# Small normalisation operations on GpSimd, W1's first pieces split by halves, the first x tile in two halves

## The chip, the cores and the metric

The kernel runs on one core of one Trainium2 chip. The metric is device microseconds of one execution. Before the change the median of three runs is 3407.81 us (3403.24 to 3411.15).

The engines are named as in the profile: PE is TensorE (PEld its weight loads), DVE is VectorE, ACT is ScalarE, POOL is GpSimd, and SP issues the transfers (SPq is its queue). Each engine executes its own instructions in the order in which the program lists them, and waits for other engines and for transfers through semaphores.

## The reference

`x` is 2048 x 1024 in float32. The kernel computes

```python
xn = layernorm(x)                        # over the last axis, eps 1e-5, no gain or bias
q, k, v = split(xn @ wqkv)               # 32 heads of 32
s = softmax(q @ k.T / sqrt(32)) @ v @ wo
h = xn @ w1 + b1                         # 1024 -> 3584
g = silu(mish(h) @ w2)                   # mish(h) = h * tanh(softplus(h))
out = x + s * g
```

Only the beginning matters here: the normalisation of `x`, the first part of `V = xn @ wv`, and the preparation of the first pieces of `w1`.

## The kernel before, in words

Every float32 matrix product is made of three products in a faster format: each operand is split into a high part (a rounded copy) and a low part (what is left), and high x high, high x low and low x high are summed. So each tile that goes into TensorE needs a copy on one engine and a subtraction (`low`) on another.

The tokens are handled in 16 tiles of 128 rows (`NT` = 16). The loop `for t in range(2, NT + 2)` is the first V pass, and a "round" below is one pass of this loop. It runs as a pipeline over tiles:

- `x_load(t)` fetches a 512 KB tile of x into one of five buffers that it shares with the raw tiles of wv. SP issues it, and waits there until the earlier user of that buffer is done.
- `ln_a(t)` on VectorE: two `bn_stats` over 512 columns each, `bn_aggr` to mean and variance, and the variance plus eps.
- `ln_r(t)` on ScalarE: the inverse square root as Ln and then Exp with scale -0.5.
- `ln_b(t)` on VectorE: four operations on 128x1 tiles that refine that root by a step of Newton's and make the bias, -mean x root.
- `ln_x(t)` on ScalarE: one 128x1024 activation that applies scale and bias.
- `ln_t(t)` on TensorE: eight 128x128 transposes into two PSUM tiles `pt`.
- `ln_c(t)`: for each half, ScalarE copies the high part from `pt` into `xc`, and VectorE subtracts the low part into it.
- `v_group(0, t)` on TensorE: 24 matmuls of 256 columns; the transposes of the next tile are placed between the eighth and the ninth (between the twelfth and the thirteenth in the first round).
- `evac()`: ScalarE copies the V tile out of PSUM, and SP issues its store.

In round t the program lists `ln_b(t)`, the matmuls of tile t-2 with the transposes of tile t-1, `ln_c(t-1)`, `ln_x(t)`, the load of tile t+4, `ln_a(t+2)`, `ln_r(t+1)`, `evac` of tile t-2, and then the preparation of w1. That order is the order on each engine's queue.

The preparation of w1 uses idle time and idle space. `w1_first(n, step)` handles the first four pieces of w1 (`W1_0` = 4), each 512 KB raw and 1 MB split. Step 0 is the load into a buffer of its own (SP); then GpSimd makes the high and the low part, four instructions over two halves of the piece; then SP moves the result to DRAM. The split piece is written into a place that isn't needed yet: the low parts of `xc[2]` and `xc[3]`, which hold tiles 8 to 11 and 12 to 15. Pieces 0 and 2 take the part that the first half of `ln_c` writes, pieces 1 and 3 the part that the second half writes, so each move must have read its place before `ln_c(8)` or `ln_c(12)` writes there. Before the change piece n is loaded in round n+2, split in round n+3 and moved in round n+5.

In rounds 9, 11, 13 and 15 SP also issues 1 MB moves of finished parts of `xc` to DRAM (`move_x`), and in rounds 13 to 15 the loads of the raw wv of the second V pass; GpSimd splits these at the end of the loop. The second V pass (512 columns, `vww`, `vwz`, `vwb`) begins after them. Behind it come the third V pass, Q and K with the preparation of w1 and w2, and then attention and the MLP, whose instructions a planner puts in order when the program is built; none of that is touched.

Of the kernel before, what the change touches and what calls it, by code (L numbers as in the profile page):

```python
# [11 lines left out]
AF = mybir.ActivationFunctionType  # L12
ALU = mybir.AluOpType
# [4 lines left out]
S, D, H, DH, F = 2048, 1024, 32, 32, 3584  # L18
P = 128
# [7 lines left out]
W1_0, W1_V = 4, 21  # L27
# [196 lines left out]
def body(ctx: ExitStack, tc: tile.TileContext, x, wqk, wv, wo, w1, b1, w2, out):  # L224
    nc = tc.nc
    x, out = x[0], out[0]
# [45 lines left out]
    def act(out_, in_, fn, bias=None, scale=1.0):  # L272
        nc.scalar.activation(out_, in_, fn, bias=zero if bias is None else bias, scale=scale)  # L273
# [4 lines left out]
    def move(out_, in_, eng=None):  # L278

        (eng or nc.sync).dma_start(out_.bitcast(F32), in_.bitcast(F32))  # L280

    def low(eng, out_, in_, high):

        eng.tensor_tensor(out_, in_, high.bitcast(F32), ALU.subtract)  # L284
# [22 lines left out]
    def v_load(i, half):  # L307
        raw = vp.tile([P, 4, 256], F32, tag="x", name=f"vraw{i}_{half}", bufs=5)
        nc.sync.dma_start(raw, wv[i][:, half * 4:half * 4 + 4])
        return raw  # L310
# [6 lines left out]
    def v_group(p, t, cut=0, between=None):  # L317
        w, first, cols = v_pass[p]
        ps = ps1.tile([P, 512], F32, tag="ps", name=f"v{first}_{t}")
        n = 0  # L320
        for k in range(KT):
            for a, b in THREE:
                if n == cut and between:
                    between()
                nc.tensor.matmul(ps[:, :cols], xc[t // 4][:, a, k, (t % 4) * P:(t % 4 + 1) * P],  # L325
                                 w(b, k), start=n == 0, stop=n == 3 * KT - 1)
                n += 1

        def evac():
            for i in range(cols // 256):  # L330
                st = vp.tile([P, 8, DH], F32, tag="vst", name=f"vst{first + i}_{t}", bufs=6)
                copy(st, ps[:, i * 256:(i + 1) * 256].rearrange("p (h d) -> p h d", d=DH))
                nc.sync.dma_start(vs[first + i][:, t], st)

        return evac
# [5 lines left out]
    def v_wide():  # L341
        tiles = [vp.tile([P, 2, 4, 512], F32R, tag="w", name="vww"),
                 w1p.tile([P, 2, 2, 512], F32R, tag="z0", name="vwz"), big.tile([P, 2, 2, 512], F32R, tag="w", name="vwb")]

        def at(b, k):
            return tiles[0][:, b, k] if k < 4 else tiles[1 + k // 2 - 2][:, b, k % 2]

        def split(i, half, raw):
            r = slice(i * 256, i * 256 + 256)
            if half == 0:  # L350
                v_split([tiles[0][:, a, :, r] for a in range(2)], raw, nc.gpsimd)
            else:
                for n in range(2):
                    v_split([tiles[1 + n][:, a, :, r] for a in range(2)], raw[:, 2 * n:2 * n + 2], nc.gpsimd)

        return at, split
# [2 lines left out]

    def x_load(t):  # L360
        xt = vp.tile([P, D], F32, tag="x", name=f"x{t}", bufs=5)
        nc.sync.dma_start(xt, x[t * P:(t + 1) * P, :])
        return xt

    first_w1 = [p.tile([P, 2, KT, P], F32, tag=tag, name=f"w1f{tag}") for p, tag in ((w1p, "z0"), (big, "w"))]

    def split_w(w, raw, job=False):
        for half in range(2):
            r = slice(half * 4, half * 4 + 4)
            p = w[half] if isinstance(w, list) else w[:, half]  # L370
            (nc.gpsimd if job else nc.vector).tensor_copy(p[:, 0], raw[:, r])
            low(nc.gpsimd if job else nc.vector, p[:, 1], raw[:, r], p[:, 0])

    def w1_first(n, step):
        t, g = xc[2 + n // 2], n % 2
        raw = first_w1[n // 2][:, g]
        w = t[:, 1, 4 * g:4 * g + 4].rearrange("p k n -> p (k n)") \
            .rearrange("p (h a k f) -> p h a k f", h=2, a=2, f=P)
        if step == 0:
            nc.sync.dma_start(raw, w1[n])  # L380
        elif step == 1:
            split_w(w, raw, True)
        else:
            move(w1s[n], w)

    xts = {t: x_load(t) for t in range(2)}
    vraw = [v_load(0, half) for half in range(2)]
    xts[2] = x_load(2)
    stat, tmps = {}, {}

    def ln_a(t):
        xt = xts[t]
        st = vp.tile([P, 2, 6], F32, tag="st", name=f"st{t}", bufs=4)
        mv = vp.tile([P, 2], F32, tag="mv", name=f"mv{t}", bufs=5)
        var = vp.tile([P, 1], F32, tag="var", name=f"var{t}", bufs=5)
        rs = vp.tile([P, 1], F32, tag="rs", name=f"rs{t}", bufs=5)
        for g in range(2):
            nc.vector.bn_stats(st[:, g], xt[:, g * 512:(g + 1) * 512])
        nc.vector.bn_aggr(mv, st)
        nc.vector.tensor_scalar(var, mv[:, 1:2], EPS, None, op0=ALU.add)  # L400
        stat[t] = mv, var, rs

    def ln_r(t):
        mv, var, rs = stat[t]
        act(rs, var, AF.Ln)
        act(rs, rs, AF.Exp, scale=-0.5)

    def ln_b(t):
        mv, var, rs = stat.pop(t)
        tmps[t] = tmp = vp.tile([P, 1], F32, tag="tmp", name=f"tmp{t}", bufs=3)  # L410
        nc.vector.scalar_tensor_tensor(tmp, rs, var, rs, op0=ALU.mult, op1=ALU.mult)
        nc.vector.tensor_scalar(tmp, tmp, -0.5, 1.5, op0=ALU.mult, op1=ALU.add)
        nc.vector.tensor_tensor(rs, rs, tmp, ALU.mult)
        nc.vector.scalar_tensor_tensor(tmp, mv[:, 0:1], -1.0, rs, op0=ALU.mult, op1=ALU.mult)
        tmps[t] = tmp, rs

    def ln_x(t):
        tmp, rs = tmps.pop(t)
        act(xts[t], xts[t], AF.Identity, bias=tmp, scale=rs)

    def ln_t(t):
        xt = xts.pop(t)
        for g in range(2):
            pts_[t, g] = pt = ps1.tile([P, 512], F32, tag="ps", name=f"pt{t}_{g}")
            for k in range(4):
                nc.tensor.transpose(pt[:, k * P:(k + 1) * P], xt[:, (4 * g + k) * P:(4 * g + k + 1) * P], ident)

    def ln_c(t):
        c, r = t // 4, slice(t % 4 * P, t % 4 * P + P)
        for g in range(2):  # L430
            k = slice(4 * g, 4 * g + 4)
            p4 = pts_.pop((t, g)).rearrange("p (k n) -> p k n", k=4)
            copy(xc[c][:, 0, k, r], p4)
            low(nc.vector, xc[c][:, 1, k, r], p4, xc[c][:, 0, k, r])

    pts_ = {}
    ln_a(0)
    ln_r(0)
    ln_b(0)
    ln_x(0)  # L440
    ln_a(1)
    ln_t(0)
    ln_r(1)
    ln_b(1)
    vw, parts_ = v_narrow(0)
    v_pass[0] = vw, 0, 256
    v_split(parts_(0), vraw[0], nc.vector)
    ln_c(0)
    v_split(parts_(1), vraw[1], nc.gpsimd)
    ln_x(1)  # L450
    ln_a(2)
    ln_r(2)
    xts[3] = x_load(3)
    x_parts = iter([(c, k) for c in range(1, NC) for k in range(0, KT, 2)])

    def move_x():
        c, k = next(x_parts)
        move(xs[c][:, :, k:k + 2], xc[c][:, :, k:k + 2])

    for t in range(2, NT + 2):  # L460
        if t < NT:
            ln_b(t)
        evac = v_group(0, t - 2, 12 if t == 2 else 8, (lambda: ln_t(t - 1)) if t <= NT else None)
        if t <= NT:
            ln_c(t - 1)
        if t < NT:
            ln_x(t)
        for m in (4, 5, 6) if t == 2 else (t + 4,):
            if m < NT:
                xts[m] = x_load(m)  # L470
        if t == 2:
            ln_a(3)
        if t + 2 < NT:
            ln_a(t + 2)
        if t + 1 < NT:
            ln_r(t + 1)
        evac()
        for step, n in enumerate((t - 2, t - 3, t - 5)):
            if 0 <= n < W1_0:
                w1_first(n, step)  # L480
        if t == NT - 3:
            vraw = {(i, 0): v_load(1 + i, 0) for i in range(2)}
        elif t in (NT - 2, NT - 1):
            i = t - NT + 2
            vraw[i, 1] = v_load(1 + i, 1)
        if 8 < t < NT and t % 2:
            move_x()
        if t == NT - 1:
            vw, split_wide = v_wide()
            v_pass[1] = vw, 1, 512  # L490
        if t >= NT - 1:
            for i, half in (((0, 0), (1, 0)), ((0, 1),), ((1, 1),))[t - NT + 1]:
                split_wide(i, half, vraw[i, half])
# [9 lines left out]
    def qk_split(f):  # L503
        qkw[f] = w_tile(f"qkw{f}")
        split_w(qkw[f], raws.pop(f))
# [904 lines left out]
    xt, yt = {}, {}  # L1410
# [23 lines left out]
    for c in range(NC):  # L1434
        for s in range(4):
            t = 4 * c + s
            if t + 4 < NT:
                start(t + 4)
            for dh in range(2):
# [5 lines left out]
                if c:  # L1445
                    n = 2 * s + dh
# [53 lines left out]
```

## Time and profile before

| | before |
|---|---|
| median of three runs | 3407.81 us |
| the profiled execution | 3404.78 us, span 3403.0 us |
| PE busy | 3350.0 us (98%) |
| DVE, ACT, POOL busy | 2683.6, 2039.2, 2727.3 us |
| mean granted TensorE clock | 0.998 |
| start of the second V pass's matmuls on `vwz` | 83.15 us |

A row of the timeline gives the start, the duration, the engine, the source line, the operation, the tile written and the tiles read, their shapes, how many instructions are merged in the row, and in brackets how long the engine was idle before it and what ended that wait. A row of the stages gives the stretch, its length, the busy time and number of instructions of PE, PEld, DVE, ACT and POOL, the granted clock, the share of the DMA engines' time and GB/s. A row of groups gives line, engine, operation, tiles, shapes and count, then busy time and mean nanoseconds of one, then the idle time before them. A row of the waits gives who waited for whom: total, times, longest.

### The profile page before, as it was taken

To read this page: it belongs to the slowest core of one execution; us is meant where nothing else is said; L and a number is where in the kernel's file an instruction comes from. 1 tells how busy PE (TensorE), PEld (TensorE's weight loads), DVE (VectorE), ACT (ScalarE), POOL (GpSimd) and SP (SyncE) were. 2 spreads that over 40 slices of the span, in tenths; PEclk is the share of its full clock that TensorE was granted. 3 is DMA by queue.
4 is the path that set the end of the run, shared out by engine and by line. 5 is a ranking of instruction groups with operands and counts; after the bars stand their busy time and mean duration, and the time that the engine had idled before them with its cause. 6 is when DMAs were issued, how large, how long until landed. Compare 5 with 4: busy or idle time off the path is not lost.

```text
span 3403.0 us, 48050 instructions
## 1 busy us (share of the span) xinstructions
PE 3350.0 (98%) x17107; PEld 2444.7 (72%) x17107; DVE 2683.6 (79%) x4462; ACT 2039.2 (60%) x3394; POOL 2727.3 (80%) x923
## 2 busy tenths in 40 slices
PE   8999999999999999999999999999999999999999
PEld 8898887767766766667777676666776666677587
DVE  6024446999999998889999988889999889896753
ACT  6112222766766667767776677667776776677621
POOL 3547662998898989999989899989988999899910
PEclk9999999999999999999999999999999999999999
DMA  8989997544555465545455564445556555546582
GB/s 285 339 307 370 369 367 243 143 137 138 154 150 148 144 192 180 149 131 153 141 157 157 182 186 137 140 141 148 149 164 198 163 149 158 150 146 193 171 306 85
DMA packets 257633, 639.87 MB, mean 188 GB/s; under 512 B 90266, under 2 KB 99482, under 8 KB 248730
## 3 DMA queue, kind: packets, MB, share of 16 engines
q1 hardware_dynamic: 254948, 628.42, 58.7%
q10 hardware_dynamic: 2448, 8.39, 0.6%
q8 instruction: 136, 2.23, 0.3%
q14 instruction: 101, 0.83, 0.1%
HBM read 474.97 MB, written 160.69 MB: 187 GB/s over the span
## 4 chain that ended last, share of the span: by engine, by line
PE 84%; DVE 7%; DMA 3%; POOL 2%; issue 2%; ACT 1%; SPq 1%; ACTq 0%; DVEq 0%; POOLq 0%
PE h L1049 16%; PE y L1190 13%; PE pv L938 13%; PE s L803 12%; PE t L890 12%; PE qk L725 8%; PE op L1317 4%; PE v L325 4%; DVE mx L809 2%; DMA kstack<-ks 1%; POOL z L919 1%; DVE yacc L1213 1%; ACT p L273 1%; PE zp L974 1%; POOL pw L284 1%
## 5 line engine op out<-in xcount | busy, mean ns | idle before, releaser
L919 POOL TENSOR_TENSOR z<-z,p 128x2048 f32<-128x2048 f32 x448 | 2066.5, 4613 | 75.0 <-ACT p L273 50.6
L273 ACT ACTIVATE p<-t,zero 128x512 f32<-128x512 f32 x2048 | 1366.5, 689 | 455.8 <-PE t L890 436.0
L809 DVE TENSOR_REDUCE mx<-s 128x1 f32<-128x512 f32 x1984 | 1283.4, 682 | 65.9 <-PE s L803 63.4
L890 PE MATMUL t<-qstack,kstack 128*128 128x512 f32 x2048 | 791.3, 394 | 1.8 <-ACT p L273 0.9
L803 PE MATMUL s<-kstack,qstack 128*128 128x512 f32 x1984 | 755.6, 397 | 14.8 <-DMA kstack<-ks 7.5
L1049 PE MATMUL h<-xr,w 128*128 128x512 f32 x2016 | 676.6, 390 | 1.4 <-DVE aw L284 0.6
L1213 DVE TENSOR_TENSOR yacc<-yacc,y 128x512 f32<-128x512 f32 x728 | 492.6, 680 | 36.8 <-PE y L1190 33.3
L803 PEld LDWEIGHTS s<-kstack,qstack 128*128 128x128 f32 x1984 | 366.8, 188 | 160.8 <-issue 26.8
L890 PEld LDWEIGHTS t<-qstack,kstack 128*128 128x128 f32 x2048 | 382.0, 188 | 126.5 <-issue 28.5
L938 PE MATMUL pv<-p,v 128*32 128x512 f32 x4096 | 466.0, 595 | 1.0 <-ACT p L273 0.6
L1049 PEld LDWEIGHTS h<-xr,w 128*128 128x128 f32 x2016 | 377.6, 188 | 84.1 <-DVE aw L284 2.1
L725 PE MATMUL qk<-xc,qkw 128*128 128x512 f32 x1536 | 351.3, 389 | 0.3
L725 PEld LDWEIGHTS qk<-xc,qkw 128*128 128x128 f32 x1536 | 288.0, 188 | 60.8 <-DVE mx L607 1.2
L938 PEld LDWEIGHTS pv<-p,v 128*32 128x32 f32 x4096 | 119.9, 109 | 276.4 <-issue 247.6
L919 POOL TENSOR_TENSOR z<-p,p 128x2048 f32<-128x2048 f32 x32 | 147.8, 4620 | 159.5 <-PE zp L974 107.1
L1190 PE MATMUL y<-w,az 128*128 128x512 f32 x672 | 232.1, 395 | 4.7 <-POOL az L284 1.7
L1190 PE MATMUL y<-w,ay 128*128 128x512 f32 x672 | 227.2, 391 | 3.4 <-ACT ay L276 1.4
L1190 PE MATMUL y<-w,ax 128*128 128x512 f32 x672 | 225.1, 391 | 2.2 <-DVE ax L284 0.7
L1049 PE MATMUL h<-xc,w 128*128 128x512 f32 x672 | 225.7, 391 | 0.0
L950 DVE TENSOR_TENSOR o<-o,pv 128x512 f32<-128x512 f32 x96 | 65.9, 687 | 117.0 <-PE pv L938 112.9
L1190 PEld LDWEIGHTS y<-w,az 128*128 128x128 f32 x672 | 125.1, 189 | 37.1 <-DVE yacc L1213 3.1
L1190 PEld LDWEIGHTS y<-w,ay 128*128 128x128 f32 x672 | 125.2, 188 | 33.2 <-DVE yacc L1213 3.5
(134 smaller groups left out, 3627.8 us busy)
## 6 DMA issues: line engine op xcount, KB each, us to landing
w<-w2s SPq DMA_DIRECT2D x392, 512.0 KB
w<-w1s SPq DMA_DIRECT2D x224, 512.0 KB
w2s<-pw SPq DMA_DIRECT2D x98, 512.0 KB
qstack<-qs SPq DMA_DIRECT2D x96, 256.0 KB
kstack<-ks SPq DMA_DIRECT2D x96, 256.0 KB
w1s<-w1h SPq DMA_DIRECT2D x34, 512.0 KB
x<-in_A_x_dram SPq DMA_DIRECT2D x32, 512.0 KB
qs<-qst SPq DMA_DIRECT2D x32, 512.0 KB
```

The source lines that it names most:

```text
L273: nc.scalar.activation(out_, in_, fn, bias=zero if bias is None else bias, scale=scale)
L325: nc.tensor.matmul(ps[:, :cols], xc[t // 4][:, a, k, (t % 4) * P:(t % 4 + 1) * P], w(b, k), start=n == 0, stop=n == 3 * KT - 1)
L725: nc.tensor.matmul(ps, w[:, k // 4, a, k % 4], xc[c][:, b, k], start=n == 0, stop=n == 3 * KT - 1)
L803: nc.tensor.matmul(sp_, qst[h % 3][:, qt * P:(qt + 1) * P], kst[h % 3][:, kc * 512:(kc + 1) * 512], start=True, stop=True)
L809: nc.vector.reduce_max(tiles["mx"][:, qt, kc:kc + 1], tiles[qt, kc], axis=AX.X)
L890: nc.tensor.matmul(tp, kst[h % 3][:, kt * P:(kt + 1) * P], qst[h % 3][:, c * 512:(c + 1) * 512], start=True, stop=True)
L919: nc.gpsimd.tensor_tensor(zs[h], pts[T - 1] if kt == 1 else zs[h], pts[T], ALU.add)
L938: nc.tensor.matmul(t["b"][c * DH:(c + 1) * DH, :], vt[h][:, k, :], pts[T - kt + k][:, c * 512:(c + 1) * 512], start=k == kt - size + 1, st ...
L1049: nc.tensor.matmul(t["h"], w1t[m_][:, a, k % 4], xts_[c][:, b, k], start=i == 0, stop=i == 3 * KT - 1)
L1190: nc.tensor.matmul(t["y"], acts[B, kind][:, p, half * 256 + s * P:half * 256 + (s + 1) * P], w2t[m_][:, q], start=i == 0, stop=i == 2)
L1213: nc.vector.tensor_tensor(ya, ya, t["y"], ALU.subtract)
L1317: nc.tensor.matmul(ps[t, dh], ohl[t // 4, k][:, a, s * P:(s + 1) * P], wt[k][b][:, r], start=k == 0 and i == 0, stop=k == KT - 1 and i == 2)
```

## The change

There are three edits. From the third token tile on (`t > 1`) `ln_b` runs on GpSimd, as six operations instead of four, since the fused form of two tensors and a scalar is written out as two instructions each; the last two are the product with the mean and its negation. The first x tile is loaded as two halves of 512 columns, and its normalisation is made as two activations. And the first four pieces of w1 are taken one every two rounds: piece n is loaded in round 2n+2, its first half is split in round 2n+3 and its second half in round 2n+4, and it is moved in round 2n+6. In a round the load (step 0) and the move (step 3) are listed ahead of the splits (steps 1 and 2).

```diff
     def x_load(t):
         xt = vp.tile([P, D], F32, tag="x", name=f"x{t}", bufs=5)
-        nc.sync.dma_start(xt, x[t * P:(t + 1) * P, :])
+        for r in (slice(0, 512), slice(512, D)) if t == 0 else (slice(0, D),):
+            nc.sync.dma_start(xt[:, r], x[t * P:(t + 1) * P, r])
         return xt
...
-    def split_w(w, raw, job=False):
-        for half in range(2):
+    def split_w(w, raw, job=False, halves=range(2)):
+        for half in halves:
...
         if step == 0:
             nc.sync.dma_start(raw, w1[n])
-        elif step == 1:
-            split_w(w, raw, True)
+        elif step < 3:
+            split_w(w, raw, True, (step - 1,))
         else:
             move(w1s[n], w)
...
     def ln_b(t):
         mv, var, rs = stat.pop(t)
         tmps[t] = tmp = vp.tile([P, 1], F32, tag="tmp", name=f"tmp{t}", bufs=3)
+        if t > 1:
+            g = nc.gpsimd
+            g.tensor_tensor(tmp, rs, var, ALU.mult)
+            g.tensor_tensor(tmp, tmp, rs, ALU.mult)
+            g.tensor_scalar(tmp, tmp, -0.5, 1.5, op0=ALU.mult, op1=ALU.add)
+            g.tensor_tensor(rs, rs, tmp, ALU.mult)
+            g.tensor_tensor(tmp, mv[:, 0:1], rs, ALU.mult)
+            g.tensor_scalar(tmp, tmp, -1.0, 0.0, op0=ALU.mult, op1=ALU.add)
+            tmps[t] = tmp, rs
+            return
         nc.vector.scalar_tensor_tensor(tmp, rs, var, rs, op0=ALU.mult, op1=ALU.mult)
...
     def ln_x(t):
         tmp, rs = tmps.pop(t)
-        act(xts[t], xts[t], AF.Identity, bias=tmp, scale=rs)
+        for r in (slice(0, 512), slice(512, D)) if t == 0 else (slice(0, D),):
+            act(xts[t][:, r], xts[t][:, r], AF.Identity, bias=tmp, scale=rs)
...
-        for step, n in enumerate((t - 2, t - 3, t - 5)):
-            if 0 <= n < W1_0:
+        for step in (0, 3, 1, 2):
+            n, odd = divmod(t - 2 - step - step // 3, 2)
+            if not odd and 0 <= n < W1_0:
                 w1_first(n, step)
```

## The prediction

> **What bounds the kernel now.** I read the busy time by stage first, for where TensorE idles; then what TensorE waited for up to the end of the first V pass; then the chain of waits and the timeline there.
>
> ```profile
> core 0: us, PE busy (x) PEld busy (x) DVE busy (x) ACT busy (x) POOL busy (x), PEclk, DMA share, GB/s
> 18.73:43.66 24.93, 23.43 (x195) 22.74 (x194) 23.82 (x64) 18.59 (x37) 14.94 (x16) 1.00 0.90 312
> 43.66:58.67 15.01, 15.01 (x131) 15.00 (x129) 13.37 (x40) 12.29 (x25) 0.00 (x0) 1.00 1.02 400
> 58.67:73.84 15.17, 12.98 (x99) 12.78 (x97) 9.00 (x26) 9.70 (x20) 0.00 (x0) 0.89 0.69 233
> 83.15:580.00 496.85, 495.29 (x2359) 416.39 (x2359) 185.42 (x248) 96.27 (x184) 292.58 (x240) 1.00 0.92 335
> ...
> PE pt L426 <- ACT x L273: 9.0, 1, 9.0
> PE v L325 <- DVE xc L284: 3.6, 3, 2.2
> PE v L325 <- POOL vwz L284: 0.4, 1, 0.4
> ```
>
> From 83.15 to 580 us TensorE idles 1.6 us in 497: whatever the change does to the first 83 us is handed on one for one. In those 83 us TensorE waits 9.0 us for the first normalised tile and 3.6 us in three pieces for VectorE. The edits all lie there, so at most some 13 us can be won, less what no edit touches.
>
> The chain of waits from 18 to 45 us lies almost wholly on VectorE. TensorE's own pace is visible in the undisturbed tiles; the start of each tile's transposes (the second and third row) marks it.
>
> ```profile
> by line: DVE st L398 31.2%; DVE xc L284 26.7%; DVE rs L413 8.8%; DVE tmp L411 6.8%; DVE mv L399 5.7%; DVE tmp L414 4.6%; PE v L325 4.5%; DVE var L400 4.0%; DVE tmp L412 3.7%; PE pt L426 3.2%; issue 2.9%
> ...
> 47.50 1.03 PE L426 MATMUL pt<-ident,x 128*128 128x128 f32 x8
> 51.24 1.03 PE L426 MATMUL pt<-ident,x 128*128 128x128 f32 x8
> ...
> 18.83 1.03 PE L426 MATMUL pt<-ident,x 128*128 128x128 f32 x8
> 27.29 1.03 PE L426 MATMUL pt<-ident,x 128*128 128x128 f32 x8
> 73.94 1.04 PE L426 MATMUL pt<-ident,x 128*128 128x128 f32 x8
> ```
>
> TensorE needs 51.24 - 47.50 = 3.74 us a tile. From tile 2 (18.83) to tile 4 (27.29) two tiles take 0.98 us over that. From tile 4 to tile 10 (51.24) six tiles take 23.95 us, 1.51 over 6 x 3.74 = 22.44; from tile 10 to tile 15 (73.94) five take 22.70, 4.00 over 18.70. What was lost in the latter is one late transfer and the clock behind it:
>
> ```profile
> 50.45 1.23 SPq L362 DMA_DIRECT2D x<-in_A_x_dram  x1
> 61.03 1.29 DVE L398 BATCH_NORM_STATS2 st<-x 128x6 f32<-128x512 f32 x2 [2.52 <-DMA x<-in_A_x_dram]
> 64.15 1.65 PE L325 MATMUL v<-vw,xc 128*128 128x256 f32 x6 [2.19 <-DVE xc L284]
> 65.60 1.89 PE L426 MATMUL pt<-ident,x 128*128 128x128 f32 x8
> ```
>
> Tile x14 is issued at 50.45 and used at 61.03, behind four 1 MB moves of W1 and one of x; TensorE idles 2.19 us, and then eight transposes take 1.89 us instead of 1.03: of the 4.00 us, 4.00 - 2.19 = 1.8 is slow running after the idle.
>
> **The change, part by part.** First, x0 in halves.
>
> ```profile
> 0.74 0.86 SPq L362 DMA_DIRECT2D x<-in_A_x_dram  x2
> 4.37 1.29 DVE L398 BATCH_NORM_STATS2 st<-x 128x6 f32<-128x512 f32 x2 [2.78 <-DMA x<-in_A_x_dram]
> 7.61 1.24 ACT L273 ACTIVATE x<-x,tmp,rs 128x1024 f32<-128x1024 f32 x1 [0.86 <-DVE tmp L414]
> ```
>
> Two statistics of 0.64 us start when all of x0 is there; with halves the first can run while the second half lands: a gain between 0 (the first half lands no sooner) and 0.64. One more issue on SP (0.43 us) pushes x1 and what follows by as much, which is needed only after the first tile's chain. The split normalisation lets transposes start earlier, but the first V matmuls wait for ScalarE's later copies. I take 0.5 us, near the upper end, since transfer and statistics simply overlap.
>
> Second, the four small operations leave VectorE from tile 2 on.
>
> ```profile
> L411 DVE SCALAR_TENSOR_TENSOR tmp<-rs,var 128x1 f32<-128x1 f32 x10 | 3.1, 310 | 0.0
> L413 DVE TENSOR_TENSOR rs<-rs,tmp 128x1 f32<-128x1 f32 x10 | 3.0, 296 | 0.3
> L414 DVE SCALAR_TENSOR_TENSOR tmp<-mv,rs 128x1 f32<-128x1 f32 x10 | 1.9, 189 | 0.3
> 40.78 1.29 POOL L284 TENSOR_TENSOR xc<-w1fw,xc 128x512 fp32r<-128x512 f32 x1
> 40.94 1.15 DVE L413 TENSOR_TENSOR rs<-rs,tmp 128x1 f32<-128x1 f32 x1
> L284 POOL TENSOR_TENSOR hl<-nm,hl 128x16 fp32r<-128x16 f32 x31 | 7.0, 227 | 7.6 <-ACT hl L276 7.5
> ```
>
> VectorE then has under 3 us a tile and no longer sets the pace; also gone are waits such as L413's 1.15 us for a one-element operation, which ends with GpSimd's. That is the intended gain: the 1.51 and 0.98 us above. In its place come six dependent operations on GpSimd. Nothing of 128x1 with two inputs is there before; the nearest row is 227 ns at 128x16. With the 0.09 us that lies between GpSimd's dependent instructions (25.16 + 0.63 to 25.88, below) and a little less for the smaller shape I take 6 x 0.275 = 1.65 us, with bounds of 0.6 (six of a constant's memset on the same engine, some 0.1) and 2.3. The Trainium skill (GPSIMD Engine Reference, Performance versus the Vector engine) speaks against the move: an elementwise two-input operation costs about twice VectorE's time there. By that ratio it would be some 2.1 us, an estimate, and 0.4 more a round below.
>
> Third, and this decides: GpSimd executes in order, and ahead of `ln_b(t)` it now has half a W1 piece that must first have landed.
>
> ```profile
> 20.61 0.33 SPq L333 DMA_DIRECT2D vs<-vst  x1
> 20.98 0.43 SPq L380 DMA_DIRECT2D w1fz<-in_B_w_dram  x1
> 25.16 0.63 POOL L371 CAST xc<-w1fz 128x512 fp32r<-128x512 f32 x1 [9.98 <-DMA w1fz<-in_B_w_dram]
> 25.88 1.30 POOL L284 TENSOR_TENSOR xc<-w1fz,xc 128x512 fp32r<-128x512 f32 x1
> 27.12 0.61 POOL L371 CAST xc<-w1fz 128x512 fp32r<-128x512 f32 x1
> 25.85 1.24 ACT L273 ACTIVATE x<-x,tmp,rs 128x1024 f32<-128x1024 f32 x1 [0.67 <-DVE tmp L414]
> 52.94 1.25 ACT L273 ACTIVATE x<-x,tmp,rs 128x1024 f32<-128x1024 f32 x1
> 54.09 0.27 ACT L273 ACTIVATE rs<-var,zero 128x1 f32<-128x1 f32 x1
> 54.40 0.29 ACT L273 ACTIVATE rs<-rs,zero 128x1 f32<-128x1 f32 x1
> 54.60 0.36 ACT L276 ACTIVATE vst<-v 128x256 f32<-128x256 f32 x1
> 54.99 0.67 SPq L333 DMA_DIRECT2D vs<-vst  x1
> ```
>
> Before, nobody waits for GpSimd here, and its 9.98 us wait for the first piece is free. Afterwards the piece is loaded at the end of round 2, its first half split at the end of round 3, and `ln_b(4)` stands behind that. Piece there at 25.16 - 0.5 = 24.66; half a split (27.12 - 25.16 = 1.96) to 26.62; `ln_b` 1.65 to 28.27; `ln_x(4)` at 28.30 instead of 25.85. Transposes follow `ln_x` by 27.29 - 25.85 = 1.44: tile 4 at 29.74 instead of 27.29, **2.45 us late**. Behind `ln_x` on ScalarE stand the next tile's Ln and Exp, V's evacuation and the next copies; behind the evacuation, on SP, the next W1 load. So it is a closed round of two tiles: `ln_x` to Ln 1.15, to Exp 0.31, to evacuation 0.20, to SP's store 0.39, to the W1 load 0.37, to the piece 4.18 (25.16 - 20.98), half split 1.96, `ln_b` 1.65, `ln_x` 0.03: **10.24 us against 2 x 3.74 = 7.48**. It runs three times (tiles 4 to 6, 6 to 8, 8 to 10): tile 10 at 29.74 + 30.72 = 60.46, against 51.24. In tiles with no load pending, a half split and `ln_b` take 3.6 us, inside 3.74. The load's time is bounded by 3.6 (x0, 0.74 to 4.34) and some 5.7 in the busier DMA; 4.18 is its own row.
>
> Fourth, the moves out of the scratch come later: piece 1's in round 8, piece 3's in round 12, and rounds 9 and 13 write the second half of that scratch.
>
> ```profile
> 44.78 1.70 SPq L280 DMA_DIRECT2D w1s<-xc  x1
> 45.76 1.29 DVE L284 TENSOR_TENSOR xc<-pt,xc 128x512 fp32r<-128x512 f32 x2
> ```
>
> Before, the row at 44.78 is piece 3's move, four tiles ahead of its need; the low parts at 45.76 needed piece 1's, issued long before. Afterwards: `ln_x(8)` at 48.78, load of piece 3 at 51.20, landing 55.38, and right behind it the move, 1.05 MB at 400 GB/s = 2.6 us, to 58.0. The low part is done at 58.65, and TensorE, at the fifteenth matmul of tile 8, waits for it. Then 18 matmuls (2.2 us), and 0.8 for tile 9's low part, which VectorE makes only after 1.6 us of statistics: tile 10 at 61.65 rather than 60.46. With TensorE at 3.74 from there, tile 15 comes at 61.65 + 18.70 = 80.35. Piece 3's move costs by the same steps 0.35 directly and 0.8 behind it: 81.5. x14 is no longer late: two moves stand ahead of it, not four, and it has more time. After the stalls I count the slow running once, 1.8 (inside a round it is hidden, for there the round sets the pace): 83.3, against 73.94: **9.3 us later**. The Trainium skill (TensorE: Matmul & The Clock Gate, The HAM clock gate) says that the clock falls only after an idle window of about 3.4 us. By that, stalls of 2 to 3 us would leave the clock alone and the sum would be 7.5; the trace disagrees, with 0.89 over the stage that held a 2.19 us wait. The second V pass begins behind the same GpSimd splits as before, with the same 0.4 us.
>
> The profiled execution took 3404.78 us (span 3403.0 and 1.78 around it), 3.0 under the runs' median of 3407.81. The sum on it is 3414.1; I move the difference to the median: 3417.
>
> **Rivals.** *All is won.* The pieces land before GpSimd reaches them, and moves in time. Then TensorE runs at 3.74 throughout: 0.5 + 0.98 + 1.51 + 4.00 = 7 us, 3401. It decides once a piece lands within 4.18 - 2.76 = 1.4 us of its issue, so that the round fits in 7.48. For it speaks that the first round starts with TensorE clearly waiting for VectorE; against it that a piece takes 4.18 us.
> *The round is short.* GpSimd's six operations take 0.6 and the load 3.6: a round is 8.6, tile 4 at 28.1, tile 10 at 53.9 (the moves then cost 1 to 2 us), no slow clock; against the 4.0 us regained at x14 this ends near +1: 3409.
> *The round is long.* Loads at 5 us or more beside the moves, operations of 0.35, slow clock twice: three rounds at 11.7 and 1.8 more: +16, 3424.
> *Later stages absorb it.* The DMA share of 0.92 up to 580 us could be a bound of its own; then nothing shows, 3408. Against it: TensorE hardly ever waits there.
>
> **How the numbers follow.** Likeliest 0.47 (own range 3411 to 3422); short round 0.25; long round 0.12; all won 0.11; absorbed 0.05. A measurement of this kernel tells about 0.2%, 6.8 us, from no change: 3401.0 to 3414.6. Slower: a fifth of the likeliest lies inside that bound, so 0.47 x 0.8 + 0.12 = 0.50. All won lies on the other edge, so half of 0.11 is faster, 0.06. Within: 0.44. The range runs from 3404 to 3425, leaving out most of "all won" and the end of the long round.
>
> **What would show it.** Right: GpSimd's casts of w1f waiting on their DMA in rounds 3, 5, 7, 9 with ScalarE's `ln_x` of tiles 4, 6, 8, 10 waiting on GpSimd; two-tile distances near 10.2 us; VectorE waiting for a W1 move ahead of the low parts of tiles 8 and 12; no wait for x14; the second pass starting near 92 us instead of 83.15. Wrong: transposes 3.74 us apart in tiles 4 to 10, or casts that find their piece there; a second pass at 76 us would mean that all is won, and a late second pass with the same end that it is absorbed.

## The result, and the profile after

The changed kernel takes 3417.39 us (median of seven runs, 3414.36 to 3420.99), beside 3406.19 us for the kernel before. The ratio is 1.0031, with a 95% interval of 1.0020 to 1.0043. The forecast was 3417 with a range of 3404 to 3425, and slower as the likeliest sign. The median of the kernel before is taken from seven runs here; the forecast was built on three of them, with a median of 3407.81.

Everything that the change moves lies in the first V pass. The first view is the busy time by stage of the changed kernel (columns as in the stages of before). The cuts lie at its own transposes of tiles 2, 8, 12 and 15 and at the second V pass.

```profile
core 0: us, PE busy (x) PEld busy (x) DVE busy (x) ACT busy (x) POOL busy (x), PEclk, DMA share, GB/s
19.67:51.84 32.17, 25.03 (x195) 24.18 (x194) 19.41 (x43) 18.55 (x37) 17.23 (x48) 0.94 0.63 217
51.84:72.28 20.44, 18.40 (x128) 17.90 (x129) 11.00 (x22) 12.99 (x27) 8.99 (x31) 0.84 0.87 326
94.41:591.00 496.59, 495.17 (x2358) 416.23 (x2358) 185.42 (x248) 95.80 (x184) 292.06 (x240) 1.00 0.92 335
...
PE pt L438 <- ACT x L273: 15.7, 5, 8.6
ACT x L273 <- POOL tmp L419: 12.4, 6, 3.9
POOL xc L372 <- DMA w1fw<-in_B_w_dram: 7.3, 2, 3.8
POOL xc L372 <- DMA w1fz<-in_B_w_dram: 6.6, 2, 3.4
```

Between tiles 2 and 8 TensorE idles 7.1 us of 32, and VectorE has become a light engine (19.4 of 32). The four rows of waits spell the new chain: GpSimd waits 13.9 us for W1's four pieces, ScalarE 12.4 us for GpSimd's last small operation, TensorE 15.7 us for ScalarE (8.6 of it the start). After 94.41 us the stage that took 497 us before takes as long again, with 1.4 us of idle TensorE (1.6 before). So the shift of the second V pass, 94.41 - 83.15 = 11.3 us, is handed on, and the medians differ by 11.2. That the two agree so closely is partly chance: a second profile of each kernel, below, gives 13.3 for the same shift.

One turn of the chain, from the timeline of the changed kernel, and then the starts of `ln_x` for tiles 6, 8 and 10:

```profile
21.86 0.42 SPq L381 DMA_DIRECT2D w1fz<-in_B_w_dram  x1
25.99 0.61 POOL L372 CAST xc<-w1fz 128x512 fp32r<-128x512 f32 x1 [3.17 <-DMA w1fz<-in_B_w_dram]
27.93 0.19 POOL L414 TENSOR_TENSOR tmp<-rs,var 128x1 f32<-128x1 f32 x1
29.30 0.19 POOL L419 TENSOR_SCALAR tmp<-tmp 128x1 f32<-128x1 f32 x1
29.53 1.24 ACT L273 ACTIVATE x<-x,tmp,rs 128x1024 f32<-128x1024 f32 x1 [3.60 <-POOL tmp L419]
30.82 1.78 PE L438 MATMUL pt<-ident,x 128*128 128x128 f32 x8 [2.71 <-ACT x L273]
...
39.85 1.24 ACT L273 ACTIVATE x<-x,tmp,rs 128x1024 f32<-128x1024 f32 x1 [1.95 <-POOL tmp L419]
50.55 1.24 ACT L273 ACTIVATE x<-x,tmp,rs 128x1024 f32<-128x1024 f32 x1 [3.88 <-POOL tmp L419]
61.00 1.24 ACT L273 ACTIVATE x<-x,tmp,rs 128x1024 f32<-128x1024 f32 x1 [2.21 <-POOL tmp L419]
```

The piece lands 4.13 us after its issue; half a split takes 1.94; the six operations take 29.49 - 27.93 = 1.56; ScalarE starts 0.04 later. That is the first piece. The three later ones land 4.37, 4.74 and 4.52 us after their issue (31.95 to 36.32, 42.28 to 47.02, 52.97 to 57.49). The two-tile rounds take 10.32, 10.70 and 10.45 us. In a second profile of the same kernel they take 10.09, 10.54 and 10.90.

The late moves, in the same timeline (each row's bracket names what ended the wait; at 59.99 it names a GpSimd operation on 128x1 tiles, of which this row needs nothing; the transfer that has to leave this place first is the move issued at 53.49, and in the run with early moves, below, the wait is gone):

```profile
53.49 0.40 SPq L280 DMA_DIRECT2D w1s<-xc  x1
59.99 0.69 DVE L284 TENSOR_TENSOR xc<-pt,xc 128x512 fp32r<-128x512 f32 x1 [5.68 <-POOL tmp L415]
60.74 3.87 PE L325 MATMUL v<-vw,xc 128*128 128x256 f32 x18 [1.92 <-DVE xc L284]
77.64 0.69 DVE L284 TENSOR_TENSOR xc<-pt,xc 128x512 fp32r<-128x512 f32 x1 [3.41 <-DMA w1s<-xc]
80.61 0.98 PE L325 MATMUL v<-vw,xc 128*128 128x256 f32 x6 [0.53 <-DVE xc L284]
94.41 1.42 PE L325 MATMUL v<-vwz,xc 128*128 128x512 f32 x5 [0.44 <-POOL vwz L284]
```

The move needs 6.5 us, VectorE stands for it, TensorE idles 1.92 us and then needs 3.87 us for 18 matmuls, where the kernel before took 2.39 (its row at 59.57).

### The profile page after: what moved, and what is told of

It reads as the page before. It is cut to its first block, busy times and chain, and to the rows that moved or that the text cites. A ratio compares the mean times of both kernels' runs of the same rounds, so it can differ in the third digit from the quotient of the medians.

```text
span 3419.2 us, 48099 instructions
## 1 busy us (share of the span) xinstructions
PE 3356.8 (98%) x17107; PEld 2448.3 (72%) x17107; DVE 2672.6 (78%) x4406; ACT 2037.7 (60%) x3395; POOL 2741.7 (80%) x1007
```

## Experiments

The mark in all of them is the start of the second V pass's matmuls on `vwz` after their wait: 83.15 before, 94.41 changed. It comes from one profile each; three kernels were profiled twice, and there the mark repeats within 0.6 us for the changed kernel, 0.6 for the one with loads, splits and moves all earlier, and 2.7 for the kernel before. What follows the mark takes 3319 to 3325 us in all the profiles, 3319.9 and 3321.5 in the two of the kernel before, 3324.8 and 3319.1 in the two of the changed one. It shows no relation to the edits, so the mark says more about them than the whole time does.

Theory A is the closed round of the prediction. Rival B says that GpSimd is simply too slow for the small operations. Rival C says that the late moves are the loss.

**The loads earlier, nothing else.** To the changed kernel:

```diff
     xts[2] = x_load(2)
+    w1_first(0, 0)
+    w1_first(1, 0)
...
-        for step in (0, 3, 1, 2):
-            n, odd = divmod(t - 2 - step - step // 3, 2)
-            if not odd and 0 <= n < W1_0:
+        for step, late in ((0, -2), (3, 6), (1, 3), (2, 4)):
+            n, odd = divmod(t - late, 2)
+            if not odd and (2 if step == 0 else 0) <= n < W1_0:
                 w1_first(n, step)
```

> The changed kernel with only W1's loads earlier: pieces 0 and 1 are loaded ahead of x3, pieces 2 and 3 in rounds 2 and 4, four rounds ahead of their split; splits and moves stay where the change put them. Times are those at which the second V pass's matmuls on vwz begin after their wait (83.15 before, 94.41 after). Theory A (a closed round: the W1 load stands behind ScalarE's evacuation, GpSimd waits for the piece, ln_b stands behind the split, ln_x behind ln_b): the casts find their pieces there, tiles 2 to 8 come every 3.74 us, tile 8's transposes at about 42 us instead of 51.84; the two late moves remain with about 2.6 and 1.2 us; second pass at 81 to 83, the whole 2 us faster than before to equal to it. Rival B (the six operations cost by themselves, since GpSimd is slow and shared with the splits, wherever the loads are): ScalarE's ln_x still waits for GpSimd in most tiles, second pass after 90, the whole within 3 us of the changed kernel. Rival C (the late moves out of the scratch are what costs): second pass at 92 or later.

From the timeline of this kernel, TensorE and the first of the two VectorE rows that wait for a move:

```profile
43.01 1.03 PE L440 MATMUL pt<-ident,x 128*128 128x128 f32 x8
46.75 1.03 PE L440 MATMUL pt<-ident,x 128*128 128x128 f32 x8
48.99 0.69 DVE L284 TENSOR_TENSOR xc<-pt,xc 128x512 fp32r<-128x512 f32 x1 [4.02 <-DMA w1s<-xc]
49.73 1.70 PE L325 MATMUL v<-vw,xc 128*128 128x256 f32 x12 [1.24 <-DVE xc L284]
83.24 1.45 PE L325 MATMUL v<-vwz,xc 128*128 128x512 f32 x5 [0.43 <-POOL vwz L284]
```

Tile 8's transposes come at 43.01 instead of 51.84, and the tiles ahead of it lie 3.74 us apart: the same six operations on GpSimd no longer hold up TensorE (ScalarE still waits for them twice, 0.43 and 0.36 us, for tiles 3 and 4). The mark goes from 94.41 to 83.24; 11.2 us belong to the loads' place. The whole was expected at 2 us under before to equal, and is 1.0012 (1.0003 to 1.0022): a miss on the slow side. The two moves cost 2.3 and 2.5 us (tiles 9 to 10 take 6.02 us, 13 to 14 take 6.27), not 2.6 and 1.2, and the kernel before was better in a second profile than in its first, as the last runs show.

**The moves one round earlier, nothing else.**

```diff
-        for step in (0, 3, 1, 2):
-            n, odd = divmod(t - 2 - step - step // 3, 2)
-            if not odd and 0 <= n < W1_0:
+        for step, late in ((0, 2), (3, 5), (1, 3), (2, 4)):
+            n, odd = divmod(t - late, 2)
+            if not odd and (0 if step == 0 else 0) <= n < W1_0:
                 w1_first(n, step)
```

> The changed kernel with only W1's moves one round earlier (round 2n+5): loads and splits as changed. Theory A: rounds of two tiles of 10.3 to 10.7 us stay from tile 4 to tile 10; VectorE no longer waits for a move ahead of the low parts of tiles 8 and 12, which is worth 2 to 4 us: second pass at 90 to 92, 7 to 9 us slower than before. Rival C: the second pass comes at 84 or sooner, the whole equal to before. Rival B: as theory A, since this edit leaves ln_b alone.

TensorE's waits in the timeline:

```profile
30.67 1.09 PE L438 MATMUL pt<-ident,x 128*128 128x128 f32 x8 [2.45 <-ACT x L273]
40.75 1.09 PE L438 MATMUL pt<-ident,x 128*128 128x128 f32 x8 [2.37 <-ACT x L273]
50.77 1.09 PE L438 MATMUL pt<-ident,x 128*128 128x128 f32 x8 [2.33 <-ACT x L273]
61.20 1.09 PE L438 MATMUL pt<-ident,x 128*128 128x128 f32 x8 [2.72 <-ACT x L273]
89.20 1.43 PE L325 MATMUL v<-vwz,xc 128*128 128x512 f32 x5 [0.44 <-POOL vwz L284]
```

Four waits, always two tiles and 10.0 to 10.4 us apart, and none behind a move. The mark is 5.2 us earlier than in the changed kernel, where 2 to 4 were expected (89.20, expected 90 to 92), and the whole 1.0026 (1.0015 to 1.0037). So rival C has a real share, larger than expected, and the smaller one.

**Only the small operations on GpSimd**, W1 and x0 as before (the new branch of `ln_b` added to the kernel before, nothing else).

> Only the move of the small operations to GpSimd; W1's pieces are loaded, split whole and moved as before, x0 is whole. Theory A: now a whole piece (3.9 us) stands ahead of ln_b in rounds 3 to 6, so tiles 4 to 7 are late, tile 7 by some 11 us; after that no piece stands in the way and TensorE runs at 3.74, regaining what was lost before at x14: second pass at 88 to 91, the whole 5 to 8 us slower than before. Tiles 9 to 15 show no ln_x waiting for GpSimd. Rival B: the loss is spread over all tiles, tiles 9 to 15 too, and is no larger than in the kernel with early loads. Rival C: no late move here, so no slower than before.

```profile
31.59 1.97 PE L436 MATMUL pt<-ident,x 128*128 128x128 f32 x8 [4.35 <-ACT x L273]
49.97 1.54 PE L436 MATMUL pt<-ident,x 128*128 128x128 f32 x8 [2.62 <-ACT x L273]
90.71 1.43 PE L325 MATMUL v<-vwz,xc 128*128 128x512 f32 x5 [0.42 <-POOL vwz L284]
```

Tile 4 (31.59) to tile 7 (49.97) are late, tile 7 by 11.0 us. From tile 8 at 55.32 to tile 15 at 81.50 the distance is 7 x 3.74. The ratio is 1.0020 (1.0011 to 1.0029). Rival B falls: tiles without a W1 piece ahead of `ln_b` lose nothing.

**Only W1's schedule**, with the small operations on VectorE and x0 whole.

> Only W1's schedule (pieces every two rounds, halves, later moves); the small operations stay on VectorE, x0 is whole. Theory A: GpSimd's wait for a piece is free again, since nothing of the normalisation stands behind it, so tiles 4 to 8 are paced by VectorE as before (within 1 us of before at tile 8's transposes, 43.76); the late moves hold up the low parts of tiles 8 and 12, 3 to 5 us at the first with the slow clock behind it and 1 to 3 at the second; x14 is not late (4 us regained): second pass at 83 to 87. Rival B (the small operations on GpSimd are all of the loss): second pass no later than before, 79 to 83.

```profile
52.27 4.05 PE L325 MATMUL v<-vw,xc 128*128 128x256 f32 x18 [3.67 <-DVE xc L284]
71.08 1.74 PE L325 MATMUL v<-vw,xc 128*128 128x256 f32 x12 [1.95 <-DVE xc L284]
74.00 1.65 PE L325 MATMUL v<-vw,xc 128*128 128x256 f32 x6 [1.19 <-DVE xc L284]
90.23 1.43 PE L325 MATMUL v<-vwz,xc 128*128 128x512 f32 x5 [0.41 <-POOL vwz L284]
```

The tiles up to 8 are on time (42.60 against 43.76), as expected. The moves cost far more than expected, and the mark of 90.23 lies outside the expected 83 to 87: tiles 9 to 10 take 9.30 us and 13 to 15 take 13.64, together 11.7 over TensorE's pace. Slow running is part of that (4.05 us for 18 matmuls after the first wait). The ratio is 1.0033 (1.0021 to 1.0044), as much as the whole change. Each half of the change is slow by itself; together they do not add up. A likely reason is that the rounds spread the tiles in time and so give the moves more of it: from tile 8's transposes to the low part that follows the move 8.93 us pass here and 8.15 in the changed kernel, from tile 12's 6.68 and 5.36. No run tests this by itself.

**Loads, splits and moves all earlier**, small operations on GpSimd, x0 whole: as in the run with early loads, with `((0, -2), (3, 4), (1, 2), (2, 3))` for the steps.

> Small operations on GpSimd and W1 split by halves as changed, x0 whole as before, loads early as in the run with early loads, splits in rounds 2n+2 and 2n+3, moves in round 2n+4. Theory A: no wait for a piece, none for a move; TensorE at 3.74 us a tile from tile 2 on, tile 15's transposes at 67 to 68 us (73.94 before); x14 not late, since three moves instead of four stand ahead of it, further apart; second pass at 76 to 77.5, the whole 6 us (0.18%) faster than before. Rival B: second pass later than before, the whole 2 us or more slower than before. Rival C: as A, but with the loads adding nothing to it.

> The kernel with early loads, splits and moves and the small operations on GpSimd, once more, beside the next run on one chip. Second pass at 76.5 to 78; 3 to 6 us faster than before, as in its first run (ratio 0.9989). If it comes out at 1.000, the first run's gain was not one.

A stage of its first run, and the mark:

```profile
core 0: us, PE busy (x) PEld busy (x) DVE busy (x) ACT busy (x) POOL busy (x), PEclk, DMA share, GB/s
19.83:68.60 48.77, 48.77 (x419) 48.65 (x418) 35.51 (x76) 39.57 (x80) 27.62 (x92) 1.00 0.89 323
77.82 1.43 PE L325 MATMUL v<-vwz,xc 128*128 128x512 f32 x5 [0.43 <-POOL vwz L284]
```

From tile 2 to tile 15 TensorE is busy 48.77 of 48.77 us; in the second run it waits once, 0.37 us, for tile 3's normalisation. The marks are 77.82 (76 to 77.5 expected) and 77.19. The ratios to the kernel before are 0.9989 (0.9981 to 0.9998) and 0.9988 (0.9979 to 0.9998): 3 to 4 us faster where 6 were expected at first. Both intervals end just under 1, and a difference of the same size turns up below between two kernels whose marks agree; it is the mark, 2.7 to 6.0 us ahead of the kernel before by any pair of profiles, that carries the gain.

**The same with the small operations on VectorE** (the GpSimd branch taken out).

> The kernel with early loads, splits and moves, but with the small operations on VectorE for every tile. This parts its gain of 5.3 us at the second pass into W1's schedule and the move to GpSimd. Theory A: the move is worth what VectorE lost in tiles 3 to 10, 1 to 2.5 us, since there TensorE waits for VectorE and not in the other tiles; the schedule is worth the 3 to 4 us of x14: second pass at 79 to 80.5. Rival: all is the schedule, second pass at 77.8 as with GpSimd.

```profile
23.96 0.98 PE L325 MATMUL v<-vw,xc 128*128 128x256 f32 x6 [1.66 <-DVE xc L284]
79.27 1.43 PE L325 MATMUL v<-vwz,xc 128*128 128x512 f32 x5 [0.44 <-POOL vwz L284]
```

The mark is at 79.27 against 77.8 and 77.2, so the move to GpSimd is worth 1.5 to 2.1 us once nothing stands ahead of it, as expected. (One profile stands behind 79.27.) The whole is 0.9999 (0.9990 to 1.0008), from which no difference to before can be told.

**Only x0 in halves.**

> Only x0 in two halves, all else as before. The prediction took a gain of 0.5 us; the trace of the changed kernel instead has the first half's statistics early, the second half's at 4.96, the result no sooner, and x1 late by 0.6 us. Theory A: so here the first V matmul comes at 11.9 instead of 11.34 and the second V pass 0 to 0.6 us later than before. Rival: the first tile is 0.5 us sooner and the loss in the changed kernel came from the other edits.

VectorE's first statistics here, and then those of the changed kernel, with ScalarE's row for tile 1's root and the first V matmul:

```profile
3.58 0.69 DVE L399 BATCH_NORM_STATS2 st<-x 128x6 f32<-128x512 f32 x1 [2.00 <-DMA x<-in_A_x_dram]
4.80 0.69 DVE L399 BATCH_NORM_STATS2 st<-x 128x6 f32<-128x512 f32 x1 [0.53 <-DMA x<-in_A_x_dram]
```

```profile
4.96 0.69 DVE L399 BATCH_NORM_STATS2 st<-x 128x6 f32<-128x512 f32 x1 [0.65 <-DMA x<-in_A_x_dram]
8.10 1.29 DVE L399 BATCH_NORM_STATS2 st<-x 128x6 f32<-128x512 f32 x2 [0.53 <-DMA x<-in_A_x_dram]
9.85 0.29 ACT L273 ACTIVATE rs<-var,zero 128x1 f32<-128x1 f32 x1 [0.72 <-DVE var L401]
11.95 0.58 PE L325 MATMUL v<-vw,xc 128*128 128x256 f32 x1 [1.45 <-ACT xc L276]
```

The first half is there 0.8 us sooner, the second 0.4 to 0.6 later than the whole tile was (4.37), so the statistics end where they did. x1 now makes VectorE wait: its statistics start at 8.16 and 8.10 instead of 7.49. ScalarE lists tile 1's root ahead of the copies that the first V matmul needs, so it comes to them late too (9.85 instead of 9.23 for the root), and the first V matmul comes at 12.02 here and 11.95 in the changed kernel, 0.6 to 0.7 late, although the first tile's transposes began earlier (8.41 and 8.56 instead of 8.99). By tile 8 nothing of it is left (43.84 against 43.76); the one time taken equals that of before.

**TensorE kept busy ahead of the first tile**, to see the slow clock by itself: 26 and then 48 transposes of the identity into a PSUM tile that is not read, added to the fast kernel.

```diff
+    warm = ps1.tile([P, 512], F32, tag="ps", name="warm")
+    for i in range(48):
+        nc.tensor.transpose(warm[:, i % 4 * P:(i % 4 + 1) * P], ident, ident)
     ln_a(0)
```

> The kernel with early loads, splits and moves and the small operations on GpSimd, and 26 transposes of the identity on TensorE ahead of the first tile, into a PSUM tile that nobody reads. It tests what the slow clock costs at the beginning, where 12 matmuls take 0.25 us each and the second tile's transposes 1.9 us. If the clock follows what TensorE did just before, the first V matmuls take 0.12 us, tile 1's transposes come at 13.9 to 14.3 instead of 15.1 and take 1.0, tile 2's at 17.5 to 18 instead of 19.83, and the second pass at 75.5 to 76.3 instead of 77.82. If it follows only the time since the program began, or falls in the idle microsecond ahead of the first tile, nothing changes.

> As the run with 26 transposes of the identity ahead of the first tile, but with 48. The 26 ended at 5.97 us and TensorE then idled 2.89 us, and the first tile's transposes were slow again. 48 should end near 8.5 to 9.5 us, so that no idle time over 1 us lies ahead of the first tile. If the slow clock follows an idle time of some 2 us (as after the stalls in the changed kernel), the first V matmuls now take 0.12 us and tile 2's transposes come at 17.5 to 18.3 us instead of 19.8; second pass at 75.5 to 76.5. If the clock falls for another reason, nothing changes, or the first tile's transposes come later by what the 48 overrun.

With 48, TensorE's timeline and a stage:

```profile
8.87 1.09 PE L438 MATMUL pt<-ident,x 128*128 128x128 f32 x8 [0.33 <-ACT x L273]
11.30 0.38 PE L325 MATMUL v<-vw,xc 128*128 128x256 f32 x1 [1.34 <-ACT xc L276]
12.08 3.10 PE L325 MATMUL v<-vw,xc 128*128 128x256 f32 x11 [0.39 <-DVE vw L284]
12.00:14.00 2.00, 1.90 (x7) 1.61 (x8) 2.00 (x5) 1.81 (x2) 1.24 (x1) 0.50 0.61 193
```

The first tile's transposes are fast now (1.09 us), but waits of 1.34 and 0.39 us follow them, the granted clock is 0.50 for the matmuls, and eleven of them take 3.10 us as without the 48. With 26, even the first tile's transposes stay slow (1.97 us). The marks are 77.67 with 26 and 77.76 with 48, as without. The whole times are 0.9996 (0.9987 to 1.0005) and 0.9982 (0.9973 to 0.9991). Since both start the second V pass at about the same moment as the kernel without the transposes, the 0.14% between them comes from elsewhere, and I cannot say from where. It is also a measure of how little a difference of 0.1% in the whole time says.

**Both kernels, profiled again.**

> The kernel before, profiled a second time. All distances are read from one profile each, so this shows how well such a reading repeats. Expected: the transposes of tiles 2 to 12 within 0.5 us of the first profile (18.83 to 58.78); x14's wait, which comes from a full DMA queue, may differ; second pass at 80.5 to 83.5 us. If the mark moves by more than 3 us, the distances of single profiles are worth less than the expectations took them for.

> The changed kernel, profiled a second time. If the closed round sets the pace, ln_x of tiles 4, 6, 8 and 10 again start 10.3 to 10.7 us apart; second pass at 92 to 96 us.

The kernel before, at x14 and at the mark:

```profile
62.46 0.98 PE L325 MATMUL v<-vw,xc 128*128 128x256 f32 x6 [0.41 <-DVE xc L284]
80.48 1.43 PE L325 MATMUL v<-vwz,xc 128*128 128x512 f32 x5 [0.92 <-POOL vwz L284]
```

The changed kernel repeats (93.78). Tiles 3 to 12 of the kernel before repeat within 0.2 us; tile 2 comes 0.84 late, outside the 0.5 expected, since the slow running at the start lasts longer (1.91 us for tile 1's transposes instead of 1.58). The kernel before has a mark of 80.48: x14 came in time to cost 0.41 us of idle TensorE instead of 2.19, and no slow clock followed. So the 4.0 us that the first profile lost there is an upper case, and 0.8 (70.77 - 51.30 - 18.70, tiles 10 to 15) is another.

## Why the prediction was right, point by point

- *The closed round.* Right in mechanism and size. Forecast 10.24 us, measured 10.32, 10.70 and 10.45. Its terms: half a split 1.96 forecast and 1.94 measured, `ln_b` 1.65 and 1.56, the way from `ln_x` over ScalarE and SP to the next load 2.42 and 2.4. The landing, 4.18, was a little short for the rounds: 4.37, 4.74 and 4.52. It fits only the first piece, 4.13. Loading earlier removes 11.2 us; taking `ln_b` off GpSimd removes the rounds as well.
- *x0 in halves.* Wrong in sign: 0.5 us gained was forecast, none came, and x1 was 0.6 late. This step rested on transfer and statistics overlapping; the second half landed later than the whole tile had. It also took x1 as needed only after the first tile's chain, and x1's statistics were needed at once. `ln_x(4)` starts 1.2 us too late (29.53, forecast 28.30). The missing gain is 0.5 of that. Another 0.8 is the first piece landing at 25.99 instead of 25.16, of which x1 is 0.6 and longer slow running at the start the rest (1.91 us for tile 1's transposes instead of 1.58, as the second profile of the kernel before has it without the change). The shorter `ln_b` takes 0.1 off.
- *The late moves.* Right in mechanism. From `ln_x(8)` to the landed move 9.2 us were forecast and 9.4 measured (50.55 to 59.99). The second was 0.35 + 0.8 and measured 0.63 + 0.53 of idle time, with tile 14 coming 1.7 over TensorE's pace. The slow running, counted once with 1.8, comes to 1.9 behind the first move (18 matmuls in 3.87 us instead of 2.39, and tile 11 comes 0.39 over the pace); behind tiles 4 and 8 it is there too, but inside the rounds, where it is hidden, as forecast. Undone alone, the moves are worth 5.2 us against the 4.1 forecast with the slow clock (1.2, 1.15 and 1.8).
- *VectorE relieved.* Right: with everything in time TensorE waits 0 to 0.4 us between tiles 2 and 15, and the move itself is worth 1.5 to 2.1 us. That is a little less than the 2.5 us forecast, which is what the first profile of the kernel before loses from tile 2 to tile 10; its second profile loses 1.7.
- *x14 no longer late.* Right that it isn't late; mis-sized as a gain. The 4.0 us were read from one profile of before, and a second one shows 0.8.
- *The sum.* 9.3 us forecast for the second V pass, 11.3 measured between the first profiles and 13.3 between the second ones, against 11 in the whole time. Of the 2.0 us missing between the first profiles 1.1 lie ahead of tile 4's transposes (30.82, forecast 29.74), where the wrong sign at x0 counts, and 0.5 at the second move. The oversized x14 is not among them, since in that pair the kernel before did lose its 4.0 us; it counts between the second ones, where it makes 3.2 (4.0 - 0.8) of the 4.0 us missing. That the total of 3417 was hit within 0.4 us is luck: the shift was 1.9 us too small (9.3 of 11.2 between the medians), and the median of three runs to which it was added was 1.6 us too high (3407.81 against 3406.19), so the two errors nearly cancel.
- *The rivals.* "All is won" described what the kernel with early loads and moves does, not this one. Its deciding point, a piece that is there when GpSimd reaches it, was the right one, and its gain of 7 us was put about twice too high: the whole time shows 3 to 4.

## What to carry to other kernels

Work moved to an idle engine is not free when that engine idles because it waits for a transfer: what stands ahead of it in the queue, and what that waits for, becomes part of the moved work's path. Follow the path on until it comes back to itself; where it closes, as here over ScalarE's evacuation, SP's queue and the load, its length sets the pace and can be added up from the profile of before. The cure was not to move the work back but to issue the loads earlier, and to free the scratch earlier.

## What the runs showed of the hardware that was not expected

The slow clock does not follow the length of the last idle time alone. TensorE ran slowly after waits of 1.92, 2.71 and 3.00 us in the changed kernel (granted clock 0.50 to 0.51 at 63 to 65, 32 to 34 and 53 to 55 us) and after 1.34 and 0.39 close together in the run with 48 transposes. It ran at full speed after four waits of 2.33 to 2.72 us in the run with early moves (granted clock 1.00, eight transposes in 1.09 us). The Trainium skill (TensorE: Matmul & The Clock Gate, The HAM clock gate) gives an idle window of about 3.4 us that runs freely. A free-running window would agree with equal waits having unequal effects, though no run here shows the window itself; that a whole window of 3.4 us must be idle does not agree with the slow running after 1.92 us, with TensorE busy without a gap for 7 us ahead of it.

On GpSimd each of the six 128x1 operations takes 0.19 us, and they start 0.27 to 0.28 apart; VectorE's four take 0.15 to 0.22 where nothing delays them and start 0.19 to 0.26 apart. At this size the two engines are nearly alike operation by operation, far from the factor of two that the prediction weighed.

A 512 KB transfer cut in two by columns, so that each row of 4 KB becomes two of 2 KB, brought the first half 0.8 us sooner and the second 0.4 to 0.6 us later than the whole had come.
